# Last-stage weights decoded between the second block's own, kept in DRAM as float32, with two plain chunks and seven sevens

## The chip, the cores and the metric

The kernel runs on one core of a Trainium2 chip. The metric is the device time of one execution in microseconds (us), as the median of three runs. TensorE is called PE below, VectorE DVE, ScalarE ACT, GpSimd POOL and SyncE SP.

## The reference, cut to what matters

An attention over a small memory is followed by two dense blocks. All arrays are float32 in the reference; the weights arrive as 64-bit numbers, of which the kernel makes float32 itself ("decoding").

```python
x = attention(q, k, v, phi)                  # 2304 tokens x 512
x = (x @ w_a) * (x @ w_b) @ w_out            # first block, 512 -> 1536 -> 512
h = x @ w_in                                 # second block, 512 -> 2048
g = h * (1.0 / (1.0 + np.exp(-1.702 * h)))
out = g @ moe2_w_out                         # last stage, 2048 -> 512
```

## The kernel before, in words

Every product is made to nearly float32 accuracy by splitting both operands into a high and a low part: ACT copies the value into the reduced format (`hi`), DVE or POOL subtracts that from the value (`lo`), and PE multiplies three times (`PASSES`: high by high, low by high, high by low). The split is `hi_lo`; its subtraction is `combine`, which goes to DVE or POOL. All splits therefore carry line 339 (the subtraction) or 345 (the high part), and are told apart by their tiles.

The order of the instructions on each engine is not written by hand: streams (Python generators) ask an `Order` object for an engine, a slot or a mark, and its table of estimated times and the priorities (`PR`, `PT` and so on) decide which stream is recorded next. On the chip each engine then runs its own list strictly in that order.

The second block ("second block" below is `x @ w_in`) runs as 24 rounds (`quad`, line 1281), each of seven products of a Strassen-like scheme (`seven` makes the operands). Its weights come in 8 groups (`("in", g)`), two raw pieces each. A raw piece of 512 KB is loaded by SP into one of two `raw` tiles, decoded by two ACT instructions (lines 438 and 442) and one DVE instruction (line 444) into a `dm` tile, and combined and split into `win`. The result of a round is gated by ACT (line 1333) and stored to DRAM (`g2d`).

The last stage reads `g2d` back in 9 chunks of 256 tokens. A chunk is done in one of two ways:

- plain (`proj2`, line 1482): two tiles of 128 tokens, 16 slices of the weights, three passes, 96 matmuls of 512 columns. It needs the split weights `wo2[0..15]` and split pieces of the chunk (`sb`, 128x512 each, four for each tile). There are six slots for split pieces, `sb_s`. `QUARTERS` lists the pieces: a quarter of the weights (4 slices) at a time over all plain tiles.
- seven products (`proj2_seven`, line 1513): 168 matmuls of 256 columns. It needs also the 32 combined and split weight blocks `wt` (8 pairs, four blocks each; `load_pair` reads two 128x512 slices of float32 weights from `w2d` in DRAM, `combine` makes four 128x256 sums one after the other, and `split_t` splits each), and 14 split pieces of sums for each chunk (`sums_gated`).

Before, chunks 0 to 2 are plain and run side by side (`NF = 3`), chunk 3 is plain too (`NQ = NS = 4`), and chunks 4 to 8 use seven products. The 16 raw pieces of the last weights (`("o2", c)`) come after all those of the second block. Each is decoded, split into `wo2[c]` straight from the decode tile, and stored to `w2d`. The `wt` work waits for the mark `decoded`, which is set when `wo2[15]` is ready. The wide loads (1 MB) of the first seven-product chunk go to memory that the plain pieces occupy, so they wait until the last plain piece is split (mark `front`).

Of the kernel before, what the change touches and what calls it, by code (L numbers as in the profile page):

```python
# [15 lines left out]
HI, LO = 0, 1  # L16
# [8 lines left out]
PR = 30  # L25
PT = 28
MBN = 8
# [17 lines left out]
PY = 5  # L45
RX = 12

FIRST = (
# [147 lines left out]
def tile_mem_attention_moe_moe2(  # L196
# [127 lines left out]
    def f32(ap):  # L324
        return ap.bitcast(F32)
# [73 lines left out]
    def rows(w, r0, nr, c0, cw):  # L399
        return w[r0 * P:(r0 + nr) * P, 2 * c0:2 * (c0 + cw)].rearrange("(r p) f -> p r f", p=P)  # L400
# [4 lines left out]
    for g in range(NG1):  # L405
        for r in range(2 * NHG):
            pieces.append((("wab", g, r), 0, [rows(w, r, 1, g * CW, CW) for w in (w_a, w_b)], 1))
    pieces += [(("o1", c), 0, [rows(w_o1, c, 1, 0, DM)], 1) for c in range(F1 // P)]
    for g in range(NG2):
        pieces += [(("in", g), i, [rows(w_in, 2 * i, 2, g * G2 * P, G2 * P)], 2) for i in range(2)]  # L410
    pieces += [(("o2", c), 0, [rows(w_o2, c, 1, 0, DM)], 1) for c in range(F2 // P)]
    decoded = {}
# [16 lines left out]
    def decode_piece(t, i, name, part, n, m):  # L429
# [18 lines left out]
        if name[0] == "wab":  # L448
            wt[name] = m
            od.mark(t, *name)  # L450
        elif name[0] == "in":
            decoded[name, part] = m
            od.mark(t, "decoded", name, part)
            if part == 1:
# [617 lines left out]
    yc, win, wo2 = {}, {}, []  # L1072
    win_s, hb_s, f_s, fw_s, sb_s, tb_s = Slots(), Slots(), Slots(), Slots(), Slots(), Slots()
    wo2_t, blocks = {}, []
# [93 lines left out]
    def room_last():  # L1168
# [16 lines left out]
        for p in range(F2 // P // 2):  # L1185
            od.spawn(PT, load_pair(p))
        for c, x in enumerate(views(acc, FN, 2, n), len(pieces) - 3):
            yield "mark", "raw", c
            give(f_s, [x])
        t = yield "mark", "wo2", F2 // P - 1  # L1190
        crowded()
        od.mark(t, "decoded")
        give(tb_s, [x[0].rearrange("p f j -> p (f j)").bitcast(F32) for x in raw_t])
        yield "mark", "front"
        wide = views(acc, 2 * FN, 3, n)
        give(fw_s, wide[:2])
        yield "mark", "sw", NQ, 0, A22
        give(fw_s, wide[2:])
# [3 lines left out]
        give(fw_s, views(acc, 2 * FN, 1))  # L1202
        for x in raw_t:
            give(dm_s, views(x[0].rearrange("p f j -> p (f j)").bitcast(F32), DM, 2))

# [134 lines left out]

    NF, NQ, NS, NW = 3, 4, 4, NT // NB

# [13 lines left out]
    QUARTERS = [(i, o) for o in range(0, 4 * K4, K4) for i in range(NF)]  # L1356
    QUARTERS += [(i, o) for i in range(NF, NQ) for o in range(0, 4 * K4, K4)]

    def load_gated():
        for i, o in QUARTERS:  # L1360
            s = yield "slot", f_s
            yield from gated_part(s, i, o, o + K4)
        for i in range(NQ, NW):
# [13 lines left out]
    def split_gated():  # L1377
# [8 lines left out]
        od.mark(t, "front")  # L1386
        for i in range(NQ, NW):
            yield from (split_whole(i) if i < NS else sums_gated(i))

    def split_whole(i):  # L1390
        for h in (0, 2 * K4):
            t = yield "mark", "f", i, h
            slot, f = loaded.pop(("f", i, h))
            for o in range(0, 2 * K4, K4):
                for s in range(2):
                    yield from split_part(t, f[:, o:o + K4, s * P:(s + 1) * P], "sb", i, h + o, s)
            for o in range(0, 2 * K4, K4):
                for s in range(2):
                    t = max(t, (yield "mark", "sb", i, h + o, s))
            fw_s.release(slot, t)  # L1400

# [8 lines left out]
    def sums_gated(i):  # L1410
# [21 lines left out]
        for h in (0, 2 * K4):  # L1432
# [3 lines left out]
            fw_s.release(parts[h][0], t)  # L1436

    def load_pair(p):

# [56 lines left out]
    def proj2_seven(i):  # L1496

        if i == NS:
            for p in range(2 * K4):
                yield "mark", "wt", p  # L1500
# [86 lines left out]
    def main():  # L1587
# [20 lines left out]
        for i in range(NF, NW):  # L1608
            yield from (proj2([(i, 0), (i, 1)]) if i < NS else proj2_seven(i))

# [70 lines left out]
```

## Time and profile before

| | |
|---|---|
| median of 3 runs | 746.86 us (745.54 to 747.1) |
| profiled execution | 744.51 us |
| its span, first to last instruction | 742.7 us |
| granted TensorE clock, mean | 0.999 |
| busy share of PE, DVE, ACT, POOL | 99%, 72%, 58%, 52% |
| DMA | 153.53 MB, mean 207 GB/s |

The profiled execution is 2.35 us shorter than the median of the runs. A busy PE is not a PE at its peak: matmuls overlap, so the duration of one (389 ns for 512 columns) is longer than the distance from one to the next, which has to be worked out from starts and counts.

### The profile page before, as it was taken

Reading aid. Unit: us, or ns where it says so; the run is one execution under the profiler, and the core shown is the slowest. Engines: PE = TensorE matmul, PEld = TensorE weight load, DVE = VectorE, ACT = ScalarE, POOL = GpSimd, SP = SyncE. Lnnn points to the kernel's source line nnn. Section 1 sums busy time; section 2 is a strip of 40 time slices with the busy share of each in tenths; the row PEclk is TensorE's granted clock in tenths of the full one; section 3 lists DMA queues with packets and bytes.
Section 4 is the critical chain, followed back from the end, with each engine's and each line's share of the span. In section 5 each row is a group of like instructions: output and inputs, shape, how many; then the busy total and the mean of one; then the engine's idle time right before and its main releaser. Section 6 shows DMA issues by size and latency. Waiting matters only on the chain.

```text
span 742.7 us, 14507 instructions
## 1 busy us (share of the span) xinstructions
PE 732.1 (99%) x5344; PEld 682.7 (92%) x5344; DVE 533.2 (72%) x799; ACT 430.8 (58%) x842; POOL 386.1 (52%) x347
## 2 busy tenths in 40 slices
PE   9899999999999999999999999999999999999997
PEld 8787888888889999999999999999998888999997
DVE  2987777568983447945898666666665697898884
ACT  3678664667863456546866655565656654544441
POOL 0324366447996616914998621333240296776660
PEclk9999999999999999999999999999999999999999
DMA  8998954786778966676525575544699954544411
GB/s 276 343 327 254 322 190 160 224 280 231 256 237 264 313 195 170 171 211 191 186 100 163 180 227 162 163 136 150 210 377 301 328 157 138 189 143 143 143 26 33
DMA packets 110359, 153.53 MB, mean 207 GB/s; under 512 B 8400, under 2 KB 89040, under 8 KB 110288
## 3 DMA queue, kind: packets, MB, share of 16 engines
q1 hardware_dynamic: 104928, 143.13, 60.3%
q10 hardware_dynamic: 5360, 9.47, 3.9%
q8 instruction: 42, 0.69, 0.4%
q14 instruction: 29, 0.24, 0.1%
HBM read 100.01 MB, written 52.56 MB: 205 GB/s over the span
## 4 chain that ended last, share of the span: by engine, by line
PE 92%; DMA 3%; POOL 2%; DVE 2%; SPq 1%; issue 0%; ACT 0%; DVEq 0%; POOLq 0%
PE bank L1281 24%; PE bank L844 21%; PE bank L1006 16%; PE bank L1513 14%; PE bank L1482 12%; PE bank L792 3%; DMA q<-in_q_dram 1%; PE bank L590 1%; DMA raw_p<-in_moe_w_b_dram 1%; DMA kv<-in_k_dram 1%; PE bank L509 1%; POOL w L339 1%; SPq L372 1%; POOL attn L339 1%; DVE attn L339 0%
## 5 line engine op out<-in xcount | busy, mean ns | idle before, releaser
L844 PEld LDWEIGHTS bank<-attn,eff 128*128 128x128 f32 x1152 | 154.3, 188 | 16.2 <-issue 6.1
L844 PE MATMUL bank<-attn,eff 128*128 128x288 f32 x1152 | 163.1, 298 | 0.5 <-DVE eff L812 0.5
L339 POOL TENSOR_TENSOR acc<-acc 128x512 f32<-128x512 f32 (+2 forms) x65 | 95.0, 1481 | 68.2 <-DVE w L339 27.9
L1323 DVE TENSOR_TENSOR acc<-bank,acc 128x384 f32<-128x384 f32 x168 | 89.8, 553 | 46.3 <-PE bank L1281 40.8
L339 DVE TENSOR_TENSOR w<-acc,w 128x512 fp32r<-128x512 f32 (+2 forms) x100 | 105.0, 1076 | 20.5 <-ACT w L345 20.4
L345 ACT ACTIVATE w<-acc 128x512 fp32r<-128x512 f32 (+2 forms) x129 | 74.9, 590 | 65.7 <-PE bank L1513 38.9
L345 ACT ACTIVATE attn<-acc 128x768 fp32r<-128x768 f32 (+2 forms) x80 | 61.0, 769 | 54.5 <-PE bank L1006 38.7
L1006 PE MATMUL bank<-attn,w 128*128 128x384 f32 x504 | 91.8, 335 | 0.8 <-DVE attn L339 0.7
L1006 PEld LDWEIGHTS bank<-attn,w 128*128 128x128 f32 x504 | 87.5, 188 | 2.0 <-DVE attn L339 1.4
L339 DVE TENSOR_TENSOR attn<-acc,attn 128x768 fp32r<-128x768 f32 (+2 forms) x54 | 65.6, 1225 | 31.9 <-ACT attn L345 30.8
L1333 ACT ACTIVATE acc<-acc 128x384 f32<-128x384 f32 x96 | 49.3, 524 | 44.0 <-DVE acc L1323 43.0
L339 POOL TENSOR_TENSOR attn<-acc,attn 128x768 fp32r<-128x768 f32 (+2 forms) x26 | 41.9, 1623 | 35.8 <-ACT attn L345 35.8
L1281 PE MATMUL bank<-attn,w 128*128 128x384 f32 x288 | 55.1, 334 | 0.0
L339 POOL TENSOR_TENSOR w<-dm,w 128x256 fp32r<-128x256 f32 x27 | 24.5, 908 | 57.9 <-ACT w L345 57.9
L888 POOL TENSOR_TENSOR gr<-gr 128x288 f32<-128x288 f32 x48 | 44.6, 931 | 17.0 <-issue 7.0
L339 POOL TENSOR_TENSOR w<-acc,w 128x256 fp32r<-128x256 f32 (+2 forms) x27 | 30.0, 1119 | 44.4 <-ACT w L345 44.3
L1281 PEld LDWEIGHTS bank<-attn,w 128*128 128x128 f32 x288 | 50.4, 188 | 0.0
L1006 PE MATMUL bank<-attn,w1b 128*128 128x384 f32 x252 | 47.6, 336 | 0.2 <-DVE attn L339 0.2
L339 POOL TENSOR_TENSOR sT<-sT,sm 128x576 f32<-128x576 f32 (+1 forms) x12 | 13.5, 1126 | 64.0 <-DVE sm L654 31.7
L1281 PE MATMUL bank<-w1b,w 128*128 128x384 f32 x224 | 46.2, 334 | 0.0
L1006 PEld LDWEIGHTS bank<-attn,w1b 128*128 128x128 f32 x252 | 43.8, 188 | 0.9 <-DVE attn L339 0.5
L1281 PE MATMUL bank<-w 128*128 128x384 f32 x224 | 43.8, 334 | 0.0
(185 smaller groups left out, 1448.9 us busy)
## 6 DMA issues: line engine op xcount, KB each, us to landing
acc<-g1d SPq DMA_DIRECT2D x63, 384.0 KB, 3.8
g2d<-acc SPq DMA_DIRECT2D x96, 192.0 KB, 2.0
raw<-in_moe_w_out_dram SPq DMA_DIRECT2D x24, 512.0 KB, 4.9
acc<-g2d SPq DMA_DIRECT2D x10, 1024.0 KB, 7.6
raw<-in_moe_w_in_dram SPq DMA_DIRECT2D x16, 512.0 KB, 4.3
acc<-g2d SPq DMA_DIRECT2D x16, 512.0 KB, 5.5
g1d<-gr SPq DMA_DIRECT2D x12, 576.0 KB, 4.9
g1d<-acc SPq DMA_DIRECT2D x8, 576.0 KB, 4.8
```

The source lines that it names most:

```text
L339: (nc.gpsimd if e == POOL else nc.vector).tensor_tensor(out=dst, in0=in0, in1=in1, op=op)
L345: nc.scalar.activation(out=hi, in_=src, func=AF.Copy)
L372: nc.sync.dma_start(out=dst.rearrange("p (n f) w -> p n (f w)", n=runs), in_=src)
L792: nc.tensor.matmul(ps[c][0][row(h), :], bdv[b][half, h, :], wt["wab", g, h][0][half, :], start=True, stop=True)
L844: nc.tensor.matmul(dst[:, :U], e[:, c, sw, i * CW + j * P:i * CW + (j + 1) * P], attn(b, mv, c, u * U, U), start=(n == 0), stop=(n == 3 * ...
L888: nc.gpsimd.tensor_tensor(out=dst, in0=in0, in1=in1, op=ALU.subtract)
L1006: nc.tensor.matmul(ps[0][:, :N2], w1_of(a, g, sw)[:, r * P:(r + 1) * P], b[0][:, mv, i], start=(first and q == n == 0), stop=(q == NG1 // ...
L1281: nc.tensor.matmul(ps[0][:, :N2], w[:, sw, r, :], y[mv][r], start=(n == 0), stop=(n == 5))
L1323: nc.vector.tensor_tensor(out=s[0], in0=ps[0][:, :N2], in1=x[0], op=ALU.add)
L1333: nc.scalar.activation(out=c[0], in_=c[0], func=AF.Gelu_apprx_sigmoid)
L1482: nc.tensor.matmul(ps[i, s][0], b[0][:, sw, c - o, :], wo2[c][:, mv], start=(c == n == 0), stop=(c == 4 * K4 - 1 and n == 2),)
L1513: nc.tensor.matmul(ps[name][0][:, :NB], x[0][:, sw, c, :], moving(b, h // 2 + c, mv), start=(h == c == n == 0), stop=(h > 0 and c == K4 - ...
```

## The change

Chunks 0 and 1 are plain, chunks 2 to 8 use seven products (`NF = 2`; `NQ`, `NS` and `split_whole` go). The raw pieces of the last weights are put between those of the second block (`BETWEEN`: four after group 2, three after groups 3 to 6). A decoded piece is not split any more but stored to `w2d` by SP. When all second-block pieces are decoded, `load_last` reads the 16 slices back as float32 by SP, into the four halves of the two `raw` tiles, and `split_last` splits them into `wo2`. The `wt` work has priority `PT = 4.5` instead of 28 and no longer waits for `decoded`.

```diff
-PT = 28
+PT = 4.5
+BETWEEN = (0, 0, 4, 3, 3, 3, 3, 0)
...
+    last_rows = [(("o2", c), 0, [rows(w_o2, c, 1, 0, DM)], 1) for c in range(F2 // P)]
     for g in range(NG2):
         pieces += [(("in", g), i, [rows(w_in, 2 * i, 2, g * G2 * P, G2 * P)], 2) for i in range(2)]
-    pieces += [(("o2", c), 0, [rows(w_o2, c, 1, 0, DM)], 1) for c in range(F2 // P)]
+        for _ in range(BETWEEN[g]):
+            pieces.append(last_rows.pop(0))
...
         elif name[0] == "o2":
-            c = name[1]
-            t = max(t, (yield "mark", "room", *name))
-            t, _ = yield ACT, t, act(DM)
-            nc.scalar.activation(out=wo2[c][:, HI], in_=m[0], func=AF.Copy)
-            nc.scalar.dma_start(out=w2d[c * P:(c + 1) * P, :], in_=m[0])
-            od.mark(t + 2500.0, "w2d", c)
-            t2 = yield from combine(t, wo2[c][:, LO], m[0], f32(wo2[c][:, HI]), ALU.subtract, DM)
-            dm_s.release(m, max(t + 2500.0, t2))
-            od.mark(t2, "wo2", c)
+            nc.sync.dma_start(out=w2d[name[1] * P:(name[1] + 1) * P, :], in_=m[0])
+            t = od.store(t, P * DM * 4)
+            od.mark(t, "w2d", name[1])
+            dm_s.release(m, t)
...
-    NF, NQ, NS, NW = 3, 4, 4, NT // NB
+    NF, NW = 2, NT // NB
...
+    def load_last():
+        for c in range(F2 // P):
+            yield "mark", "w2d", c
+        give(wb_s, wide_raw())
+        for c in range(F2 // P):
+            t = max((yield "mark", "room", "o2", c), (yield "mark", "w2d", c))
+            s = yield "slot", wb_s
+            nc.sync.dma_start(out=s[0], in_=w2d[c * P:(c + 1) * P, :])
+            od.load(max(t, s[1]), P * DM * 4, "o2", c)
+            od.spawn(PR, split_last(c, s))
...
+    def split_last(c, s):
+        t = yield "mark", "o2", c
+        t = yield from hi_lo(t, wo2[c][:, HI], wo2[c][:, LO], s[0], DM)
+        wb_s.release(s, t)
+        od.mark(t, "wo2", c)
...
-        t = max((yield "mark", "pair", p), (yield "mark", "decoded"))
+        t = yield "mark", "pair", p
```

The change moves what stands on DVE and ACT around the last rounds and the plain chunks. First DVE, from the late plain pieces to the first sums of the seven-product chunks. Here `w_1713<-acc 128x512` is the low part of a split piece of a chunk, a 128x256 row is `wt` work, and `acc<-acc 128x4x128` is a sum of the first seven-product chunk. Before:

```order
L339 TENSOR_TENSOR w_1713<-acc,w_1713 128x512
L339 TENSOR_TENSOR w_1713<-raw_74,w_1713 128x256
L339 TENSOR_TENSOR w_1713<-raw_73,w_1713 128x256
L339 TENSOR_TENSOR w_1713<-acc,w_1713 128x512
L339 TENSOR_TENSOR w_1713<-raw_74,w_1713 128x256
L339 TENSOR_TENSOR w_1713<-acc,w_1713 128x512 x4
L339 TENSOR_TENSOR acc<-acc 128x4x128
```

Before, the `wt` work on DVE ends with the third 128x256 row, and the last three plain pieces and the first piece of chunk 4 (`x4`) follow it without anything between. With the change, the same place:

```order
L340 TENSOR_TENSOR w_1713<-acc,w_1713 128x512
L340 TENSOR_TENSOR w_1713<-raw_74,w_1713 128x256
L340 TENSOR_TENSOR rest<-acc,rest 128x256
L340 TENSOR_TENSOR acc<-acc 128x256
L340 TENSOR_TENSOR w_1713<-acc,w_1713 128x512
L340 TENSOR_TENSOR w_1713<-raw_73,w_1713 128x256
L340 TENSOR_TENSOR w_1713<-raw_74,w_1713 128x256
L340 TENSOR_TENSOR acc<-acc 128x256 x2
L340 TENSOR_TENSOR w_1713<-acc,w_1713 128x256 x2
L340 TENSOR_TENSOR acc<-acc 128x256
L340 TENSOR_TENSOR w_1713<-acc,w_1713 128x256
L340 TENSOR_TENSOR acc<-acc 128x256
```

The second 128x512 row here is the last plain piece; `wt` work stands on both sides of it. Behind these rows come the first piece of chunk 2, the last `wt` row, a sum and the second piece of chunk 2:

```order
L340 TENSOR_TENSOR w_1713<-acc,w_1713 128x512
L340 TENSOR_TENSOR w_1713<-acc,w_1713 128x256
L340 TENSOR_TENSOR acc<-acc 128x4x128
L340 TENSOR_TENSOR w_1713<-acc,w_1713 128x512 x2
L340 TENSOR_TENSOR acc<-acc 128x4x128
```

On ACT the two first pair loads (`L1454 DMA acc<-w2d`, line 1445 before) stand behind the last gates in both kernels. With the change, what stands behind them is the high parts of five `wo2` slices, of two plain pieces, and of the first pairs:

```order
L1335 ACTIVATE acc<-acc 128x384
L1454 DMA acc<-w2d 128x2x512 x2
L346 ACTIVATE w1b<-raw_74 128x512
L346 ACTIVATE w1b<-raw_73 128x512
L346 ACTIVATE w_1713<-acc 128x512
L346 ACTIVATE w1b<-raw_73 128x512
L346 ACTIVATE w1b<-raw_74 128x512
L346 ACTIVATE w_1713<-acc 128x512
L346 ACTIVATE w1b<-acc 128x256 x3
```

The pairs' own rows (`w1b<-acc 128x256`) have moved forward to here; before, they stood behind the sixteenth slice of the last weights.

## Rows read from the trace of the kernel before

**Rows 1.** The page, parts 1 and 4: PE's share, and the chain that ended last.
```profile
PE 732.1 (99%) x5344; PEld 682.7 (92%) x5344; DVE 533.2 (72%) x799; ACT 430.8 (58%) x842; POOL 386.1 (52%) x347
...
PE 92%; DMA 3%; POOL 2%; DVE 2%; SPq 1%; issue 0%; ACT 0%; DVEq 0%; POOLq 0%
```

**Rows 2.** Busy time by stretch: two of the plain chunks, two of the sevens.
```profile
core 0: us, PE busy (x) PEld busy (x) DVE busy (x) ACT busy (x) POOL busy (x), PEclk, DMA share, GB/s
550.50:593.00 42.50, 42.50 (x189) 35.17 (x189) 23.11 (x36) 24.19 (x46) 4.74 (x5) 1.00 0.98 326
593.00:637.60 44.60, 44.60 (x199) 36.92 (x198) 35.82 (x42) 22.64 (x52) 32.11 (x34) 1.00 0.60 178
637.60:657.80 20.20, 20.20 (x170) 20.20 (x169) 19.36 (x20) 9.62 (x16) 16.20 (x11) 1.00 0.49 155
```

**Rows 3.** Timeline of PE (start us, us, engine, line): plain chunks begin, sevens begin, last group.
```profile
550.51 9.72 PE L1482 MATMUL bank<-eff,w 128*128 128x512 f32 x42
...
637.59 0.52 PE L1513 MATMUL bank<-w1b,w 128*128 128x256 f32 x3
...
737.30 1.24 PE L1513 MATMUL bank<-w1b,w 128*128 128x256 f32 x9
```

**Rows 4.** Busy time by stretch in the second block.
```profile
440.00:460.00 20.00, 20.00 (x117) 20.00 (x116) 12.52 (x23) 11.63 (x25) 5.99 (x8) 1.00 0.54 175
...
540.00:550.50 10.50, 10.50 (x62) 10.50 (x61) 9.11 (x15) 8.13 (x17) 6.85 (x6) 1.00 1.06 391
```

**Rows 5.** Groups by line (busy us, mean ns), 540 to 645 us: decoding.
```profile
L442 ACT ACTIVATE raw<-raw 128x512 uint32<-128x512 uint8 x10 | 6.5, 652 | 0.0
...
L444 DVE SCALAR_TENSOR_TENSOR dm<-dm,raw 128x512 uint32<-128x512 uint32 x7 | 4.8, 690 | 11.8 <-ACT raw L442 11.8
L438 ACT ACTIVATE dm<-raw 128x512 f32<-128x512 f32 x7 | 4.6, 662 | 11.3 <-issue 6.6 <-DMA raw<-in_moe_w_out_dram 4.6
```

**Rows 6.** Timeline of ACT, then of POOL, around the end of the second block.
```profile
550.86 0.96 ACT L1333 ACTIVATE acc<-acc 128x384 f32<-128x384 f32 x2
556.36 2.04 ACTq L1445 DMA_DIRECT2D acc<-w2d  x2
558.45 0.67 ACT L438 ACTIVATE dm<-raw 128x512 f32<-128x512 f32 x1 [6.62 <-issue]
...
562.32 0.90 POOL L339 TENSOR_TENSOR acc<-acc 128x256 f32<-128x256 f32 x1 [12.57 <-DMA acc<-w2d]
```

**Rows 7.** Timeline of DVE from the pairs to the first pieces of chunk 4.
```profile
587.57 0.42 DVE L339 TENSOR_TENSOR acc<-acc 128x256 f32<-128x256 f32 x1
589.41 0.69 DVE L339 TENSOR_TENSOR w<-acc,w 128x512 fp32r<-128x512 f32 x1 [1.42 <-ACT w L345]
...
590.37 0.96 DVE L339 TENSOR_TENSOR w1b<-acc,w1b 128x256 fp32r<-128x256 f32 x1
...
594.24 1.23 DVE L339 TENSOR_TENSOR w<-acc,w 128x512 fp32r<-128x512 f32 x1
...
623.82 2.42 DVE L339 TENSOR_TENSOR w<-acc,w 128x512 fp32r<-128x512 f32 x3
632.47 0.69 DVE L339 TENSOR_TENSOR w<-acc,w 128x512 fp32r<-128x512 f32 x1 [6.23 <-ACT w L345]
633.19 1.67 DVE L339 TENSOR_TENSOR acc<-acc 128x512 f32<-128x512 f32 x1
```

**Rows 8.** Busy time in the stretch in which the pairs are worked on.
```profile
589.40:623.80 34.40, 34.40 (x154) 28.48 (x153) 33.22 (x38) 21.58 (x52) 32.10 (x35) 1.00 0.54 157
```

**Rows 9.** Timeline of SP, then of ACT: the load for the first seven-product chunk.
```profile
626.26 5.25 SPq L1350 DMA_DIRECT2D acc<-g2d  x4
...
631.80 1.15 ACT L345 ACTIVATE w<-acc 128x512 fp32r<-128x512 f32 x2 [9.35 <-DMA acc<-g2d]
```

**Rows 10.** Line 1445, pair loads.
```profile
DMA to landing us min/median/max: 3.4/4.3/5.6
```

**Rows 11.** PE's waits, longest first (in all, times, longest).
```profile
PE bank L549 <- POOL et L540: 1.7, 1, 1.7
```

More of the change, by code (lines that the diff above doesn't have):

```diff
@@ L408, in tile_mem_attention_moe_moe2 @@
     pieces += [(("o1", c), 0, [rows(w_o1, c, 1, 0, DM)], 1) for c in range(F1 // P)]
+    last_rows = [(("o2", c), 0, [rows(w_o2, c, 1, 0, DM)], 1) for c in range(F2 // P)]
     for g in range(NG2):
         pieces += [(("in", g), i, [rows(w_in, 2 * i, 2, g * G2 * P, G2 * P)], 2) for i in range(2)]
-    pieces += [(("o2", c), 0, [rows(w_o2, c, 1, 0, DM)], 1) for c in range(F2 // P)]
+        for _ in range(BETWEEN[g]):
+            pieces.append(last_rows.pop(0))
+    assert not last_rows
     decoded = {}
@@ L453, in decode_piece @@
             od.mark(t, "decoded", name, part)
+            if (name[1], part) == (NG2 - 1, 1):
+                od.spawn(PR, load_last())
             if part == 1:
@@ L1072, in tile_mem_attention_moe_moe2 @@
     yc, win, wo2 = {}, {}, []
-    win_s, hb_s, f_s, fw_s, sb_s, tb_s = Slots(), Slots(), Slots(), Slots(), Slots(), Slots()
+    win_s, hb_s, f_s, fw_s, sb_s, tb_s, wb_s = (Slots() for _ in range(7))
     wo2_t, blocks = {}, []
@@ L1186, in room_last @@
             od.spawn(PT, load_pair(p))
-        for c, x in enumerate(views(acc, FN, 2, n), len(pieces) - 3):
-            yield "mark", "raw", c
+        for c, x in enumerate(views(acc, FN, 2, n), F2 // P - 3):
+            yield "mark", "o2", c
             give(f_s, [x])
@@ L1192, in room_last @@
         od.mark(t, "decoded")
+        for _ in range(4):
+            yield "slot", wb_s
         give(tb_s, [x[0].rearrange("p f j -> p (f j)").bitcast(F32) for x in raw_t])
@@ L1196, in room_last @@
         give(fw_s, wide[:2])
-        yield "mark", "sw", NQ, 0, A22
+        yield "mark", "sw", NF, 0, A22
         give(fw_s, wide[2:])
@@ L1202, in room_last @@
         give(fw_s, views(acc, 2 * FN, 1))
-        for x in raw_t:
-            give(dm_s, views(x[0].rearrange("p f j -> p (f j)").bitcast(F32), DM, 2))
+        give(dm_s, wide_raw())
     def split(t, dst, src, n, *key):
@@ L1356, in tile_mem_attention_moe_moe2 @@
     QUARTERS = [(i, o) for o in range(0, 4 * K4, K4) for i in range(NF)]
-    QUARTERS += [(i, o) for i in range(NF, NQ) for o in range(0, 4 * K4, K4)]
     def load_gated():
@@ L1362, in load_gated @@
             yield from gated_part(s, i, o, o + K4)
-        for i in range(NQ, NW):
+        for i in range(NF, NW):
             for o in (0, 2 * K4):
@@ L1386, in split_gated @@
         od.mark(t, "front")
[L1387 to L1400, printed above, removed]
+        for i in range(NF, NW):
+            yield from sums_gated(i)
     A21 = 7
@@ L1436, in sums_gated, with wide_raw @@
             fw_s.release(parts[h][0], t)
+    def load_last():
[8 more added lines that the diff above has]
+            od.spawn(PR, split_last(c, s))
+    def wide_raw():
+        return [y for x in raw_t for y in views(x[0].rearrange("p f j -> p (f j)").bitcast(F32), DM, 2)]
+    def split_last(c, s):
[3 more added lines that the diff above has]
+        od.mark(t, "wo2", c)
     def load_pair(p):
@@ L1496, in proj2_seven @@
     def proj2_seven(i):
-        if i == NS:
+        if i == NF:
             for p in range(2 * K4):
@@ L1608, in main @@
         for i in range(NF, NW):
-            yield from (proj2([(i, 0), (i, 1)]) if i < NS else proj2_seven(i))
+            yield from proj2_seven(i)
     def quad(g, p):
```

## The prediction

> **What bounds the kernel now.** I read the page's head and the chain that ended last first: PE is busy 99% of the span and carries 92% of the chain [rows 1], and its longest single wait in the whole program is 1.7 us, early on [rows 11]. So the time is the sum of what PE is given, and an edit pays only if it takes work from PE without making it wait. Then I read the stretches of the last stage [rows 2]: PE is full in all of them, but DVE and POOL are not the same in each. In the first half of the plain chunks POOL does 4.74 us in 42.5; in the second half, where the 32 weight blocks are made, DVE is busy 35.8 and POOL 32.1 of 44.6 us. In the first seven-product chunk DVE is at 19.4 of 20.2. There is a wide, loosely filled stretch before a full one, and the full one ends about 11 us before PE needs its result: DVE's last plain piece ends at 626.2 [rows 7], PE begins the sevens at 637.6 [rows 3]. The change takes about half of that stretch away.
>
> **What PE saves.** PE starts the plain chunks at 550.51 and the sevens at 637.59 [rows 3]: 87.08 us for 4 chunks x 96 = 384 matmuls, 226.8 ns each, 21.77 us a chunk. The last group of nine starts at 737.30 and lasts 1.24, so the five other chunks take 637.59 to 738.54, 100.95 us for 840 matmuls, 120.2 ns each, 20.19 us a chunk. One chunk that changes its form saves 1.58 us, two save 3.2 us. I take the pitch from starts and counts, since a matmul's own duration overlaps the next.
>
> **Decoding moves into the second block.** Sixteen pieces bring two ACT instructions of 0.66 us and one DVE instruction of 0.69 us each [rows 5]: 21 us on ACT, 11 on DVE, over the five groups between which they stand, some 110 us (15 rounds of 42 matmuls, 7.2 us each at 117 in 20 us [rows 4]). DVE works there 12.5 and ACT 11.6 of 20 us [rows 4]; with 2.0 and 3.8 us more per 20 neither is full, and PE covers it. Their raw loads move with them. The stretch from 540 has a DMA share of 1.06 and the first half of the plain chunks 0.98, but the second block only 0.54 [rows 2, 4]. The extra 4 MB that are read back from `w2d` (16 slices of 256 KB) fall near the end of the block, where the raw loads have gone. Cost nothing; if the cover were gone, a round would wait for its `win` weights (a rival below).
>
> **The joint before the sevens.** This is where the change can lose. PE, unhindered, would end two plain chunks at 550.51 + 192 x 0.2268 = 594.06. What is late next is the first piece of chunk 2. Its 1 MB load goes to memory that the last plain piece occupies. Before, the last plain piece was subtracted by 626.24 (623.82 + 2.42), SP issued the load at 626.26 [rows 9], ACT took the first high part at 631.80, and the first low part ended at 632.47 + 0.69 = 633.16 [rows 7]: 6.92 us from piece to piece. This costs nothing before, as PE had until 637.59. With the change, the last plain piece must be done by 594.06 - 6.92 = 587.1, or PE waits.
>
> When is it done? The pair work cannot start earlier than before by much: ACT stands still from the last gate (551.82) to 558.45, for the issue of the two pair loads, which wait for the stores of the last rounds; the first pair was worked on at 562.32 [rows 6]. Before, this stop was harmless. Now the high parts of five `wo2` slices are queued behind it on ACT, and DVE waits for these. From the first pair instruction to the last plain piece, inclusive, DVE has by the order 24 subtractions of 256 and 10 of 512. Their price hangs on POOL. With POOL idle, one of 256 takes 0.42 us and one of 512 takes 0.69; with POOL busy on the same kind of work 0.96 and 1.23 [rows 7]. Bounds: 24 x 0.42 + 10 x 0.69 = 17.0 us and 24 x 0.96 + 10 x 1.23 = 35.3 us, that is, an end at 579.3 or at 597.6. The nearest row is the same work before: 38 DVE instructions in 34.4 us beside 35 of POOL [rows 8], 0.905 us each, which gives 34 x 0.905 = 30.8 and an end at 593.1. I take 592.0, near that row: POOL has only some 22 instructions in that time against 35, so some of DVE's go at the short price (which alone would bring the end forward by up to 5 us), but there are new waits in line. Pairs 2, 3, 6 and 7 are loaded into the room of earlier pairs, 4.3 us each from issue to landing [rows 10], and the issue sits in ACT's list between high parts, so a late pair holds up a plain piece.
>
> So PE's first wait is 592.0 - 587.1 = 4.9 us. A second one follows: behind the first piece DVE does a block (0.42), a sum (1.67 [rows 7]) and the second piece (0.69), 2.8 us, while PE uses up the first piece in 12 x 0.120 = 1.4 us: 1.3 us more. After that the seven-product chunks run as before; DVE has 17 to 19 of 20 us to do in them, which fits.
>
> Here a rule of the Trainium skill can be weighed. The row on short and long prices says that the same instruction takes 0.42 or 0.96 us [rows 7]. The page VectorE: DVE Perf Modes (The TRN2 errata) gives float32 tensor-tensor work as (N + 151) / 0.96 ns, 424 ns for 256 and 691 for 512, which the rows with POOL idle confirm; by it alone the queue would take 17.1 us, PE would not wait, and the kernel would gain its 3.2 us. The GPSIMD Engine Reference (Key points) says that GpSimd shares its SBUF interfaces with VectorE and contends with VectorE instructions of two SBUF inputs; that speaks against this change, and the long rows agree with it.
>
> **The sum.** -3.2 + 4.9 + 1.3 = +3.0 us. On the profiled execution's 744.51 us (span 742.7 and 1.8 around it) this is 747.5 us. The median of the runs is 2.35 us above that execution, so the forecast for the median is **749.9 us**.
>
> **The rivals.**
>
> *DVE keeps up* (ends on the other side). The mechanism is the short price: POOL has a third less to do beside each DVE instruction, and DMA is freer after 550, so the pair loads land sooner than 4.3 us and ACT's stop of 6.6 us shrinks. For it: the 3.4 us minimum of a landing [rows 10], the 0.42 us rows. Against it: DVE's 33.2 busy of 34.4 us before [rows 8]. It decides if the last plain piece is done before 587.1; then nothing but the second wait is left, and the time is 746.86 - 3.2 + 0 to 1.3 = 743.7 to 745.0.
>
> *The wait eats the gain*: the last piece ends between 587.5 and 590.5, the wait is 1.7 to 4.7 with the second one, the result within 1.5 us of 746.9.
>
> *The queue is slow throughout*: all DVE instructions at the long price, end at 597.6, wait 10.5 + 1.3, +8.6 us, 755.5. For it: long rows were the rule while both worked. Against: POOL's smaller share.
>
> *A second-block round waits for its weights.* The groups share two raw tiles and few `dm` tiles with the new pieces, and by the order the last high part of group 3 stands one round later than before. It costs only if it slips by a further round (7.2 us); DVE and ACT have 7 and 8 of 20 us free [rows 4]. Price 1 to 5 us on top, 748 to 755.
>
> *PE's clock falls in the wait.* The granted clock is 1.00 in every stretch [rows 2], but no row shows a PE wait of 5 us, so no row shows what one does. If it fell to half, each 1.4 us piece of the first products would take 2.9 us; two such pieces add 2.9 us, 752.8. TensorE: Matmul & The Clock Gate of the Trainium skill (What's actually happening) says that an idle engine goes back to half the clock; no run here shows it.
>
> **How the numbers follow.** What a measurement of this kernel can tell from no change is about 0.2%, 1.5 us. The forecast's mechanism with an end of the last plain piece later than 590.5 has 0.45; the slow queue, a late round or a fallen clock 0.12 together; so slower has 0.57. The cancelled gain has 0.20. DVE keeping up has 0.23. The range reaches from 743.7, where nothing waits, to 754.0, which leaves out the far end of the slow queue and of the late rounds. The forecast's own range, for an end at 590.5 to 594.5, is 748.4 to 752.4.
>
> **What would show it.** Right: 192 matmuls of line 1482 at 227 ns and 1176 of line 1513 at 120; a PE wait of 3 to 6 us between the two, released by ACT or DVE, with the load from `g2d` ahead of it and the last plain piece's subtraction ahead of that; a small second one behind; ACT idle for some 6 us at 552; no new PE waits between 380 and 550. Wrong: PE running from the plain chunks into the sevens without a gap (then the short price held), several 1 us waits inside the plain chunks instead (then pieces, not the load, were late), or a wait within the second block.

## The result, and the profile after

The changed kernel takes 750.13 us (median of 5 runs, 749.62 to 750.53) against 746.86 (745.54 to 747.10): ratio 1.0055, 95% interval 1.0039 to 1.0071. It is slower by 3.3 us, which is clear of the noise. The 746.86 rests on three executions; measured again beside the experiments (17 to 23 executions each time), the kernel before has medians of 745.31 to 746.84. The profiled executions differ by more: 750.13 (span 748.3) against 744.51 (span 742.7), 5.6 us. The rows below are of the profiled ones. Its page, parts 1 and 4:

```profile
PE 732.1 (98%) x5488; PEld 688.2 (92%) x5488; DVE 549.1 (73%) x825; ACT 434.6 (58%) x852; POOL 410.9 (55%) x363
...
PE 22%; DMA 4%; DVE 4%; ACT 1%; issue 1%; POOL 1%; ACTq 0%; SPq 0%; DVEq 0%
```

PE's busy time is the same as in [rows 1] although it has two chunks in the cheaper form. The 22% can't be set against the 92% of [rows 1]: the shares add up to a third, as the page follows this chain back only to 497.65 us. What it shows is where the chain leaves PE (start us, us, what):

```profile
561.93 6.82 DMA acc<-w2d
...
601.12 0.61 DVE w L340
601.78 142.62 PE bank L1522 x1174
```

From the end back to 601.78 the chain is PE. From there back to the landing of a pair's load at 568.75 it is DVE's list, with a few rows of ACT between. PE's timeline has the waits (start us, us, engine, line; in brackets the idle time ahead of a row and what ended it). The second block, the plain products, the sevens and the last group:

```profile
375.69 1.03 PE L1283 MATMUL bank<-eff,w 128*128 128x384 f32 x5
...
552.70 0.63 PE L1491 MATMUL bank<-eff,w 128*128 128x512 f32 x2
...
584.70 11.75 PE L1491 MATMUL bank<-w1b,w 128*128 128x512 f32 x51
600.89 0.51 PE L1522 MATMUL bank<-w1b,w 128*128 128x256 f32 x2 [4.44 <-ACT w L346]
601.78 0.58 PE L1522 MATMUL bank<-w1b,w 128*128 128x256 f32 x1 [0.38 <-DVE w L340]
...
743.15 1.24 PE L1522 MATMUL bank<-w1b,w 128*128 128x256 f32 x9
```

The busy time by stretch, with the granted clock as the third column from the end and the DMA share behind it; the first row answers to one of [rows 4]:

```profile
440.00:460.00 20.00, 20.00 (x117) 20.00 (x117) 13.11 (x24) 14.52 (x32) 8.19 (x10) 1.00 0.73 232
...
375.69:552.70 177.01, 175.97 (x1009) 174.58 (x1009) 127.13 (x222) 115.29 (x249) 86.07 (x91) 1.00 0.71 232
...
596.40:600.90 4.50, 0.06 (x2) 0.01 (x1) 4.50 (x7) 3.06 (x8) 4.31 (x5) 1.00 1.08 364
600.90:606.00 5.10, 4.72 (x25) 4.51 (x26) 5.10 (x7) 4.87 (x10) 3.09 (x2) 0.67 0.76 226
```

Read these as an account from [rows 3]. The plain products begin at 552.70 and not at 550.51: +2.2. Two chunks in the cheaper form: -3.2. At 226.8 ns each, 192 plain matmuls end at 596.25; the sevens begin at 600.89: +4.6. From there 1176 matmuls at 120.2 ns would end at 742.24; the last ends at 744.39 (743.15 + 1.24): +2.15, of which 0.38 is a second, short wait. The other 1.8 lie at 600.9 to 606, where PE is busy and gets 25 matmuls done in 5.1 us, at a mean granted clock of 0.67. The sum is +5.8, as the spans say (+5.6).

What stands ahead of the first wait, in the timelines of ACT, POOL, DVE, SP and ACT again, answers to [rows 6, 7, 9]. A row with a count can hold two shapes and shows the first: the `x2` at 601.05 is the first piece's low part and a 128x256 block.

```profile
558.34 3.96 ACTq L1454 DMA_DIRECT2D acc<-w2d  x2
562.34 1.15 ACT L346 ACTIVATE w1b<-raw 128x512 fp32r<-128x512 f32 x2 [6.68 <-DMA acc<-w2d]
...
598.20 2.64 POOL L340 TENSOR_TENSOR w<-acc,w 128x256 fp32r<-128x256 f32 x3
...
566.02 0.41 DVE L340 TENSOR_TENSOR acc<-acc 128x256 f32<-128x256 f32 x1
...
592.97 0.85 DVE L340 TENSOR_TENSOR w<-acc,w 128x512 fp32r<-128x512 f32 x1 [0.31 <-ACT w L346]
...
601.05 2.10 DVE L340 TENSOR_TENSOR w<-acc,w 128x512 fp32r<-128x512 f32 x2
603.07 0.68 DVE L340 TENSOR_TENSOR acc<-acc 128x512 f32<-128x512 f32 x1
603.67 2.38 DVE L340 TENSOR_TENSOR w<-acc,w 128x512 fp32r<-128x512 f32 x2
...
593.84 0.99 SPq L1352 DMA_DIRECT2D acc<-g2d  x2
...
600.22 1.44 ACT L346 ACTIVATE w<-acc 128x512 fp32r<-128x512 f32 x3
```

ACT stands still for 6.7 us behind the last gate, over the two pair loads; the last plain piece is done at 593.82, SP issues the load at 593.84, and ACT takes the first high part of the sevens at 600.22. The pairs' work begins on DVE at 566.02.

### The profile page after: what moved, and what is told of

It reads as the page before. It is cut to its first block, busy times and chain, and to the rows that moved or that the text cites. A ratio compares the mean times of both kernels' runs of the same rounds, so it can differ in the third digit from the quotient of the medians.

```text
span 748.3 us, 14926 instructions
## 1 busy us (share of the span) xinstructions
PE 732.1 (98%) x5488; PEld 688.2 (92%) x5488; DVE 549.1 (73%) x825; ACT 434.6 (58%) x852; POOL 410.9 (55%) x363
## 5 line engine op out<-in xcount | busy, mean ns | idle before, releaser
L340 POOL TENSOR_TENSOR acc<-acc 128x512 f32<-128x512 f32 (+2 forms) x80 | 118.8, 1507 | 60.0 <-DVE w L340 38.9
L340 DVE TENSOR_TENSOR w<-acc,w 128x512 fp32r<-128x512 f32 (+2 forms) x118 | 125.2, 1089 | 16.8 <-ACT w L346 16.7
L346 ACT ACTIVATE w<-acc 128x512 fp32r<-128x512 f32 (+2 forms) x146 | 84.8, 588 | 77.6 <-PE bank L1522 55.1
L1325 DVE TENSOR_TENSOR acc<-bank,acc 128x384 f32<-128x384 f32 x168 | 87.4, 550 | 31.6 <-PE bank L1283 17.8
L346 ACT ACTIVATE attn<-acc 128x768 fp32r<-128x768 f32 (+2 forms) x84 | 62.5, 752 | 55.7 <-PE bank L1007 39.6
L1007 PEld LDWEIGHTS bank<-attn,w 128*128 128x128 f32 x504 | 87.5, 188 | 2.0 <-DVE attn L340 1.4
L340 POOL TENSOR_TENSOR w<-dm,w 128x256 fp32r<-128x256 f32 x33 | 30.0, 914 | 59.5 <-ACT w L346 59.5
L1335 ACT ACTIVATE acc<-acc 128x384 f32<-128x384 f32 x96 | 46.9, 517 | 17.3 <-DVE acc L1325 16.9
L1283 PEld LDWEIGHTS bank<-attn,w 128*128 128x128 f32 x288 | 50.4, 188 | 0.5 <-ACT acc L1318 0.5
L1522 PE MATMUL bank<-attn,w 128*128 128x256 f32 x336 | 50.1, 285 | 0.0
L340 POOL TENSOR_TENSOR w<-acc,w 128x256 fp32r<-128x256 f32 (+2 forms) x26 | 27.1, 1052 | 32.8 <-DVE dm L448 18.4
L1522 PEld LDWEIGHTS bank<-attn,w 128*128 128x128 f32 x336 | 45.0, 194 | 0.0
```

What stands on the lines that cost most here:

```text
L340: (nc.gpsimd if e == POOL else nc.vector).tensor_tensor(out=dst, in0=in0, in1=in1, op=op)
L346: nc.scalar.activation(out=hi, in_=src, func=AF.Copy)
L1007: nc.tensor.matmul(ps[0][:, :N2], w1_of(a, g, sw)[:, r * P:(r + 1) * P], b[0][:, mv, i], start=(first and q == n == 0), stop=(q == NG1 // ...
L1283: nc.tensor.matmul(ps[0][:, :N2], w[:, sw, r, :], y[mv][r], start=(n == 0), stop=(n == 5))
L1325: nc.vector.tensor_tensor(out=s[0], in0=ps[0][:, :N2], in1=x[0], op=ALU.add)
L1335: nc.scalar.activation(out=c[0], in_=c[0], func=AF.Gelu_apprx_sigmoid)
```

## The experiments

Each kernel is the changed one with the edit shown. To tell the parts apart I take three figures from each trace: how long the second block is (from its first product to the first plain one), how long the rest is (from there to the end of the span), and what PE waits for at the joint. Before: 174.7 and 192.2. After: 177.0 and 195.6. With two plain chunks and nothing lost, the rest would be 192.2 - 3.2 = 189.0. The ratio is to executions of the kernel before that were measured together with the run: medians of 746.84 (e1 to e4), 745.31 (e5 to e8), 745.59 (e9 to e11) and 746.34 (e12). The parts are of one profiled execution each.

| run | time, us | ratio to before (95%) | second block | rest | PE's waits at the joint |
|---|---|---|---|---|---|
| e1_early | 754.75 | 1.0111 (1.0094 to 1.0128) | 176.6 | 199.1 | 0.1, 2.2, 3.2, 0.8 |
| e2_filler | 751.95 | 1.0075 (1.0054 to 1.0096) | 177.4 | 194.2 | 0.4, 0.3 |
| e3_three_plain | 745.10 | 0.9983 (0.9969 to 0.9997) | 175.0 | 190.5 | none |
| e4_rows_behind | 767.64 | 1.0289 (1.0268 to 1.0310) | 174.9 | 191.1 | none; 21.9 ahead of the plain products |
| e5_thin_rows | 750.24 | 1.0058 (1.0040 to 1.0076) | 174.7 | 194.2 | 3.2, 0.4 |
| e6_third_pair | 758.35 | 1.0164 (1.0144 to 1.0184) | 177.8 | 201.8 | 0.6, 0.6, 3.3, 5.3 |
| e7_no_pair_lows | 746.13 | 0.9996 (0.9983 to 1.0009) | 176.4 | 189.1 | 0.1 |
| e8_three_spread | 746.13 | 0.9997 (0.9984 to 1.0010) | 174.7 | 190.5 | none |
| e9_spread | 753.27 | 1.0095 (1.0078 to 1.0111) | 175.9 | 197.6 | 5.9, 0.7 |
| e10_vector_alone | 747.86 | 1.0023 (1.0010 to 1.0036) | 177.2 | 191.1 | 0.1, 0.2, 0.7, 0.2 |
| e11_alone_and_spread | 745.38 | 1.0000 (0.9984 to 1.0015) | 175.6 | 188.8 | none |
| e12_alone_third_late | 746.08 | 0.9995 (0.9982 to 1.0009) | 174.7 | 190.6 | 0.1, 0.8, 0.2 |

### e1: the load ahead of the last plain piece

```diff
-        give(f_s, views(acc, FN, 1, n + 2 * FN))
+        give(f_s, views(acc, FN, 2, n))
...
-        give(fw_s, wide[:2])
-        yield "mark", "sw", NF, 0, A22
-        give(fw_s, wide[2:])
+        give(fw_s, wide[:1])
...
+    def room_wide(wide):
+        for k in (1, 2):
+            for j in range(2):
+                yield "mark", "sb", NF - 1, 4 * k, j
+            give(fw_s, [wide[k]])
```

> The last plain pieces go to the lower memory, so that the two 1 MB loads of the first seven-product chunk need no memory of the last plain piece and can be under way before it is split. Theory A (the wait at the joint is the load that stands behind the last plain piece, 593.84 to 600.2): TensorE's wait of 4.4 us falls to under 1 us, the granted clock stays at 1.00 there, the second wait of 0.4 goes; 750.1 - 4.4 - 0.4 - 1.7 = 743.6, between 743 and 745.5. Theory B (VectorE and GpSimd are themselves late by then, and would be as late with the operands loaded): the low parts of the first product start where they do now, about 601, the wait stays over 3 us and the time at 749 to 750.5.

Theory A fell. Theory B holds in kind and not in size: the time is 4 us above its range. The sevens do begin without a wait, at 596.12, and then PE stands inside the first product (PE, then POOL, then a stretch of this run with the granted clock third from the end; its lines are two higher):

```profile
601.16 0.51 PE L1524 MATMUL bank<-w 128*128 128x256 f32 x2 [2.24 <-POOL w L340]
604.92 0.58 PE L1524 MATMUL bank<-w 128*128 128x256 f32 x1 [3.25 <-ACT w L346]
606.29 0.79 PE L1524 MATMUL bank<-w 128*128 128x256 f32 x2 [0.80 <-POOL w L340]
...
598.21 2.90 POOL L340 TENSOR_TENSOR w<-acc,w 128x256 fp32r<-128x256 f32 x3
601.08 3.16 POOL L340 TENSOR_TENSOR acc<-acc 128x256 f32<-128x256 f32 x3
604.20 2.04 POOL L340 TENSOR_TENSOR w<-acc,w 128x256 fp32r<-128x256 f32 x2
...
602.00:612.00 10.00, 6.29 (x27) 6.00 (x28) 9.96 (x11) 3.81 (x8) 7.35 (x7) 0.51 0.55 157
```

What is late are the weight blocks of the last pairs, 128x256 rows: low parts end at 601.11 (PE goes on at 601.16) and 606.24 (606.29), and between them, at 604.92, PE gets the high part of a block whose sum POOL ends at 604.24. The first product needs a block of every pair. In the changed kernel the last such row on POOL ends at 598.20 + 2.64 = 600.84, where PE's wait ends too. So two things were late by the same amount, the load behind the last piece and the pairs, and the trace names only the last of them. In e1 the pairs come 5.4 us later: DVE has first sums to do before the pairs are finished, and ACT issues the load of the last pair at 595.64 instead of 591.89. The clock adds to the loss: it stays at half for some 10 us, where the changed kernel is back at 1.00 from 606 on (rows under e2). So e1 shows which operands were late, and not what an early load alone is worth.

### e2: work for PE in the wait

```diff
+        t, ps = yield PE, 0.0, 220, bank_m
+        for _ in range(34):
+            nc.tensor.matmul(ps[0][:, :NB], wo2[0][:, HI, :P], wo2[0][:, HI, :NB], start=True, stop=True)
+        bank_m.release(ps, t)
         for i in range(NF, NW):
             yield from proj2_seven(i)
```

> 34 products of 256 columns on operands already there, into a bank nobody reads, between the last plain product and the first of the seven: 34 x 0.12 = 4.1 us of TensorE work inside its wait of 4.4. The sevens' operands are as late as before. Theory A (the granted clock falls because TensorE stood still, 0.50 at 602 to 604, and this costs about 1.7 us behind the wait): the first sevens run at 1.00, the time is 750.1 - 1.7 = 748.4. Theory B (the thin stretch behind the wait is operands that come late, not the clock): no change, 749.7 to 750.5.

The clock in 2 us steps, first of the changed kernel, then of this run:

```profile
602.00:604.00 2.00, 2.00 (x10) 2.00 (x11) 2.00 (x3) 1.77 (x5) 1.03 (x2) 0.50 0.53 124
604.00:606.00 2.00, 2.00 (x15) 2.00 (x14) 2.00 (x3) 2.00 (x5) 1.50 (x1) 0.73 0.87 289
606.00:608.00 2.00, 2.00 (x19) 2.00 (x18) 2.00 (x4) 1.12 (x3) 1.27 (x1) 1.00 1.07 384
```

```profile
600.00:602.00 2.00, 2.00 (x18) 1.88 (x17) 2.00 (x4) 2.00 (x6) 1.43 (x2) 1.00 1.08 337
602.00:604.00 2.00, 1.64 (x12) 1.29 (x11) 2.00 (x3) 1.70 (x5) 0.83 (x1) 1.00 0.55 111
604.00:606.00 2.00, 1.69 (x14) 1.63 (x14) 2.00 (x3) 2.00 (x5) 1.60 (x1) 1.00 1.00 325
```

What PE still waits for in this run:

```profile
603.55 0.50 PE L1522 MATMUL bank<-w 128*128 128x256 f32 x2 [0.36 <-ACT w L346]
604.37 0.86 PE L1522 MATMUL bank<-w 128*128 128x256 f32 x5 [0.31 <-DVE w L340]
```

That PE stood still is what lowered the clock: with work in the wait it stays at 1.00. From the first seven to the last, less the waits in it, the changed kernel takes 143.1 us (743.15 + 1.24 - 600.89 - 0.38) and this run, whose last group also lasts 1.24 and starts at 742.82, 142.0 (less 601.41, 0.36 and 0.31), against 141.35 at the pitch of [rows 3]. The fall cost 1.1 to 1.8 us. The rest of the execution is 1.4 us shorter, as theory A has it. The median of 751.95 is above the ranges of both theories. This profile is the fastest of six executions (749.82 to 755.13); the five others ran at a mean clock of 0.997 or 0.998 against 1.000, so it fell somewhere in them too, and no trace shows where. Shown for the clock in one execution, open for the time.

### e3: three plain chunks

```diff
-    NF, NW = 2, NT // NB
+    NF, NW = 3, NT // NB
```

> Three chunks plain side by side and six in sevens: 65.3 us of cover for the pairs and the splits instead of 43.5. Theory A (the pairs, the splits and the load need a fixed time of about 41 us plus 8 us for the third chunk's pieces plus 6 to 7 us for the load, about 57 us behind the block's end): no wait at the joint and no fall of the clock, the second block still ends 2.2 us late, 1.6 us of the saving lost: 750.1 - 6.5 + 1.6 = 745.2, between 744 and 746.5. Theory B (VectorE and GpSimd work through the pieces no faster than TensorE through the plain products, so that the wait moves along): a wait of 3 to 5 us stays and the time is 751 to 752.

Theory A, to 0.1 us in the time. One part was wrong: the second block is not late any more, although the rows stand in it as before. That asked for an explanation, which e12 gives.

### e4 and e5: which part of the rows delays the second block

e4 has `BETWEEN = (0, 0, 0, 0, 0, 0, 0, 16)`. e5 loads an eighth of each row:

```diff
                 dst = s[0][:, i * m:(i + 1) * m, :]
+                if pieces[n][0][0] == "o2":
+                    dst, src = dst[:, :m // 8], src[:, :, :m // 4]
```

> All sixteen last-stage rows decoded behind the second block's own, as the kernel before had them, the detour over DRAM kept. Theory A (the rows in between delay ScalarE and VectorE in the second block's middle, and so TensorE): the second block ends at about 550.5 instead of 552.7, and the small waits around 484 to 509 are gone; the rows come back from DRAM later, so that a wait of up to 10 us may stand at the start of the plain products or at the joint: 748 without one, 750 to 758 with one. Theory B (the block's later end has to do with the stores and the loads of the detour, wherever they are): the block ends at 552 or later.

> Of each of the sixteen last-stage rows only an eighth is loaded (64 KB for 512 KB; the decoding works on whatever else stands in its tile, so the last stage's weights are not the reference's). All instructions of the engines stay. Theory A (the second block ends late because 8 MB more go through the DMA queue beside it: its share is 0.74 at 466 to 514 against 0.45 before, and the block's own rows land late, 5.9 us): the block ends at 550.5 to 551.3 and the time is 748 to 749. Theory B (the decoding itself, 2 us of ScalarE and VectorE for each row in the line ahead of what TensorE waits for): the block ends at 552.3 or later and the time is 749.6 to 750.6.

In e4 the block has its old length, as theory A has it, and PE then waits 21.9 us for the rows to come back from DRAM, twice what I had expected at most; the time is 10 us above the range. In e5 all instructions of ACT and DVE remain, and so do the stores to `w2d` and the loads from it; seven eighths of the raw loads go, and the block takes 174.7 us: the decoding alone delays nothing. The time did not follow (750.24 lies in theory B's range), since this execution's joint still waits 3.2 us and the second block began 3.0 us later than after (the last section has the place where it fell behind).

### e6: a place for a third pair

```diff
-        give(tb_s, views(acc, 2 * DM, 2))
+        give(tb_s, views(acc, 2 * DM, 2) + views(acc, 2 * DM, 1, n + FN))
...
-        for c, x in enumerate(views(acc, FN, 2, n), F2 // P - 3):
+        for c, x in enumerate(views(acc, FN, 1, n), F2 // P - 3):
```

> A third place for a pair's 512 KB, in memory that stands unused there, so that three pairs are loaded ahead instead of two. Theory A (the joint waits for the pairs; VectorE and GpSimd stand without work between the first pairs and the next, GpSimd 573 to 577, because the third pair can't be loaded): about 3 us of that idle time goes, the wait falls from 4.4 to 1 to 2 us, with it some of the clock's fall: 746 to 748.5. Theory B (from the first pair on the two engines have work all the time, so that it is their rate alone): no change, 749.5 to 750.5.

758.35 us, 8 us above both ranges. This says nothing of either theory: as the edit stands, the third place comes back into use for a late pair after its memory has been given to the first 1 MB load, so that part of the operands is overwritten. PE waited 3.3 and 5.3 us there.

### e7 and e10: the work of VectorE and GpSimd

```diff
     def split_t(t, dst, src, p, i):
-        t = yield from hi_lo(t, dst[:, HI], dst[:, LO], src, DM // 2)
+        t, _ = yield ACT, t, act(DM // 2)
+        nc.scalar.activation(out=dst[:, HI], in_=src, func=AF.Copy)
```

> The low parts of the 32 combined blocks are not computed (the products that use them multiply what the memory holds). This takes 32 instructions of 0.9 us from VectorE and GpSimd, some 14 us of each, and leaves every load, store and product. Theory A (the joint waits for the work of VectorE and GpSimd): no wait at the joint and no fall of the clock, 750.1 - 4.8 - 1.7 = 743.6, between 743 and 745. Theory B (the joint waits for transfers: the pairs' loads that need the places of earlier pairs, and the 1 MB load): the wait stays at 2 us or more, 746.5 or more.

```diff
-        both = {POOL: Lengths.pool * pool(n), DVE: Lengths.both * dve(n)}
+        both = {DVE: dve(n)} if Lengths.alone else {POOL: Lengths.pool * pool(n), DVE: Lengths.both * dve(n)}
...
         short()
+        Lengths.alone = True
...
-        crowded()
```

> In the last stage every subtraction and low part goes to VectorE, none to GpSimd. An operation on 128x256 starts 0.34 us after the one before it on VectorE while GpSimd is idle, and 0.88 while GpSimd works too, so that the two together need 0.44 for each. Theory A (the joint is late by the two engines' rate, and they slow each other): 64 x 0.34 + 16 x 0.60 + 5 x 0.60 = 34 us from 563, the last at 597 to 598 instead of 600.8; the wait falls to 1 to 2 us and the clock hardly falls: 745.5 to 747.5. Theory B (GpSimd's share is a real help): VectorE has 29 more operations to do and the joint waits longer: 751 to 756.

Theory A at the joint in both, and both times above its range. e7's rest is 189.1, so next to nothing is lost at the joint. Its time is 2.5 us above the 743.6 that I expected (the late second block is already in that figure): in the profiled execution the block began 2.7 us later, and the two shortest of its twelve executions, at a mean clock of 1.000, took 743.48 and 743.82. e10 does all the work and loses 2.1 us at the joint instead of 6.6; its 747.86 is 0.4 above theory A's range and 3 below theory B's. Its edit also drops `crowded()`, which lengthens times in the table that orders the lists, so that their order changes too. The price itself is read from ten microseconds among the pairs, first of the changed kernel, then of e10:

```profile
580.00:590.00 10.00, 10.00 (x46) 8.29 (x45) 10.00 (x12) 6.20 (x16) 10.00 (x11) 1.00 0.10 38
```

```profile
580.00:590.00 10.00, 10.00 (x45) 8.28 (x45) 10.00 (x27) 7.36 (x19) 0.00 (x0) 1.00 0.45 151
```

DVE and POOL together did 23 instructions, DVE alone 27, in each case four of 128x512 and the others of 128x256. The groups by line of e10 in that stretch give 0.42 us for one of 128x256 and 0.68 for 128x512, where DVE beside POOL took 0.96 and 1.23 [rows 7]:

```profile
L342 DVE TENSOR_TENSOR raw<-raw 128x256 f32<-128x256 f32 x8 | 3.3, 419 | 0.0
L342 DVE TENSOR_TENSOR w<-acc,w 128x512 fp32r<-128x512 f32 x4 | 2.7, 682 | 0.0
```

DMA traffic is not what makes the difference: its share is 0.10 in the slow stretch and 0.45 in the quick one.

### e8, e9 and e11: the rows spread over six groups

```diff
-BETWEEN = (0, 0, 4, 3, 3, 3, 3, 0)
+BETWEEN = (0, 2, 3, 3, 3, 3, 2, 0)
```

e8 has it with three plain chunks, e9 alone, e11 with e10's edit.

> Three plain chunks, and the sixteen rows spread over six groups of the second block (0, 2, 3, 3, 3, 3, 2, 0) instead of five. Theory A (the block's later end comes of too much in too short a time): it ends within 0.5 us of the kernel before (550.5), the time is 744 to 744.8. Theory B (each row costs its part wherever it is put, or the early rows delay groups that have no slack): 745 to 747.

> The changed kernel with its sixteen rows spread over six groups of the second block, (0, 2, 3, 3, 3, 3, 2, 0) instead of (0, 0, 4, 3, 3, 3, 3, 0), and nothing else. Theory A (four rows in a group are more than the queue can carry beside that group's own loads): from its first product to its end the second block takes 174.7 us as before the change, not 177.0, the joint stays as it is: 750.1 - 2.3 = 747.8. Theory B (the rows cost the block the same wherever they are put): 177 us, 749.6 to 750.5.

> Both edits of the two runs beside it. If both theories A hold and the two losses have nothing to do with each other, the gains add: 750.1 - 2.3 - 3 to 4.5 = 743.3 to 744.8, faster than the kernel before. If only one holds, its own figure.

The block's delay goes from 2.3 to 1.2 us in e9 and 0.9 in e11. But in all three PE waits 1.5 us for POOL just ahead of the second block, at about 370, where it waited 0.5, and e9's joint came out worse, 5.9 us; why, stays open. e9's 753.27 is above both theories; the spreading is no cure by itself. In e8 the block has its old length (theory A) and the time lies in theory B's range; it tells nothing of the spreading, as e3 had lost nothing either. e11 misses the 743.3 to 744.8 of added gains: 745.38 is the time of the kernel before (1.0000). Its profiled execution is the shortest of the study, 743.24, with a rest of 188.8; its twelve runs reach up to 749.25.

### e12: one load out of the queue

With e10's edit:

```diff
-        give(f_s, views(acc, FN, 3, 2 * AN))
+        give(f_s, views(acc, FN, 2, 2 * AN))
+        yield "mark", "g2", (NG2 - 2, 0), 0, 0
+        give(f_s, views(acc, FN, 1, 2 * AN + 2 * FN))
```

> VectorE alone as in e10, and the last of the three memories that are free early for the gated sums is given out late in the second block. With two plain chunks the third load, of the first chunk's second quarter, stands in SP's line at 452.3 to 457.05 and waits for gated sums still on their way to DRAM; with three chunks (e3) that place went to the third chunk's first quarter, at 405, and its second block took 175.0 us instead of 177.0. Here the load stands behind the last of the second block's rows. Theory A (this load holds up the rows queued behind it, and so ScalarE, VectorE and TensorE at 476 to 516): the second block takes 174.7 to 175.2 us from its first product to its end, against 177.2 in e10; 747.9 - 2.2 = 745.7 in the median, 743 to 743.5 where the clock does not fall at 30 us. Theory B (the rows' own transfers delay it, this load is one more among them): 176.5 to 177.3 us, 747 to 748.5 in the median.

Theory A, in the block and in the time. SP's list of the changed kernel with ACT's wait that follows, and then of e12 (its lines are two to four higher, and its second block began 2.5 us later), and last ACT's wait in e5:

```profile
451.41 0.89 SPq L1337 DMA_DIRECT2D g2d<-acc  x1
457.05 0.37 SPq L1352 DMA_DIRECT2D acc<-g2d  x1
...
458.49 0.48 SPq L373 DMA_DIRECT2D raw<-in_moe_w_in_dram  x1
...
464.55 0.67 ACT L442 ACTIVATE acc<-raw 128x512 f32<-128x512 f32 x1 [5.54 <-DMA raw<-in_moe_w_in_dram]
```

```profile
453.96 3.87 SPq L1341 DMA_DIRECT2D g2d<-acc  x2
457.92 0.39 SPq L465 DMA_DIRECT2D w2d<-dm  x1
458.36 0.44 SPq L375 DMA_DIRECT2D raw<-in_moe_w_in_dram  x1
...
462.74 0.67 ACT L444 ACTIVATE acc<-raw 128x512 f32<-128x512 f32 x1 [1.53 <-DMA raw<-in_moe_w_in_dram]
```

```profile
465.94 0.66 ACT L444 ACTIVATE acc<-raw 128x512 f32<-128x512 f32 x1 [5.45 <-DMA raw<-in_moe_w_in_dram]
```

The row at 457.05 is the load of a plain piece. SP stands 4.7 us at it, until the gated sums that it reads have reached DRAM, and it puts 512 KB more into the queue ahead of the next raw pieces; ACT, whose list has the decoding ahead of the gates, stands 5.5 us and not 1.5. PE loses its 2.3 us in small pieces between 476 and 516 (by counts of matmuls in steps of 10 us from the block's start). The stop of ACT is not enough by itself: in e5, which has the load in the same place, it is as long (5.45 us), and the block loses nothing. It takes the load and the full rows together; e12 takes away the one, e5 the other. How the stop reaches PE was not followed row by row. `QUARTERS` lists the pieces by quarter over all plain chunks, so with three of them the third free memory goes to the third chunk's first quarter, which is ready early; with two it goes to the second quarter of the first chunk. All profiled executions with that load there and full rows in between lost 0.9 to 3.1 us in the block; e3, e8 and e12, without it, 0.0 to 0.3.

## Why the prediction came out as it did

**The saving per chunk** was right: two chunks, 3.2 us, by starts and counts.

**"Cost nothing" for the decoding in the second block** failed, by 2.3 us in the profiled execution. It was one of the rivals, but with the wrong cause (and its range of 748 to 755 does not follow from its price: 1 to 5 us on top of 749.9 are 750.9 to 754.9): I looked for a round that slips by a list position, and at busy shares of ACT and DVE, 11.6 and 12.5 of 20 us [rows 4], which still had room afterwards. I read the DMA share of 0.54 [rows 4] as cover, and did not add up what would come to it; the same stretch now shows 0.73. And I did not follow SP's list past the moved pieces: it was the shorter list of plain pieces that put a waiting load among them, and that load and the rows together made the delay.

**The first wait** was right in size, 4.9 forecast and 4.6 measured: the last plain piece was done 41.1 us behind the block's end (593.82), where I had 41.5. In part errors cancel here. The pairs' work began 13.3 us behind the block's end (566.02) and not 11.8, and DVE's 34 instructions took 27.8 us and not 29.7. From the last plain piece to the first low part of the sevens it was 7.9 us (601.73) and not 6.9, but PE began with the high part, at 600.89. The forecast's account of the wait was only half of it. The load behind that piece was one of two limits, and e1 shows that taking it away gains nothing, for the pairs were just as late. Both go back to the term on which the argument turned, the long price of DVE beside POOL, and e7 and e10 confirm that one. The GPSIMD Engine Reference of the Trainium skill (Key points) says that GpSimd shares its SBUF interfaces with VectorE and contends with VectorE instructions of two SBUF inputs; the 0.42 us of e10 without POOL and the 0.96 beside it agree, though no run shows the interfaces themselves.

**The second wait**, of 1.3 us for the second piece, did not come. The 0.38 us at 601.78 belong to the first piece: PE had begun with its high part alone and waits for its low part. Behind that DVE did a block, a sum and the second piece's low part (from 603.67), as I had said; but PE was at half clock and used up the first piece more slowly. At full clock the second wait is there: 0.36 us for the high part and 0.31 for the low part in e2, 0.76 and 0.22 in e12. So its mechanism was right, and its size is 0.7 to 1.0 us.

**PE's clock** was a rival with "no row shows what a wait of 5 us does". It fell to 0.50, that is to 1.2 of 2.4 GHz, and cost 1.1 to 1.8 us, less than the 2.9 that I had reckoned. TensorE: Matmul & The Clock Gate of the Trainium skill (What's actually happening) says that an idle engine goes back to half the clock; the rows after the wait agree, and e2, without the idle time, stays at full speed.

**The median.** The forecast of 749.9 is 0.2 us from the measured 750.13, but not for its own reasons alone. On the profiled execution the sum gave 747.5, and 750.13 was measured; the 2.6 us between are the block (+2.2), the clock (+1.8), two waits smaller by 1.2 in all, and 0.25 less from the last matmul to the span's end. I had added 2.35 us for the distance of the profiled execution from its median. By the mean clocks that distance belongs to a fall of the clock at 30 to 40 us (below), which the profiled execution of the changed kernel did not have although it is the median itself. So 2.6 us left out and 2.35 us too much cancel: that the forecast came so near is luck. In the changed kernel the mean clock does not tell the times apart: 749.79 to 750.53 us at 0.998, 749.62 and 750.39 at 0.995.

## What to carry to other kernels

Add a moved load to the queue that it is moved into, together with whatever changes its place there because a list got shorter; a busy share that looks free on the engines says nothing of what stands in line at SP. When two engines slow each other down, count what they finish together in a stretch, not how busy they are: here one of them alone was faster. And when the trace names one releaser for a wait, ask what else ended within the same tenth of a microsecond before removing it. With e10's and e12's edits the change comes back from 1.0055 to 0.9995 of the time before, no gain that can be measured; three plain chunks do as well (0.9983, interval 0.9969 to 0.9997) with a single number changed.

## What the runs showed of the hardware that was not expected

Two instructions at a time on DVE and POOL were slower than one after the other on DVE: 23 against 27 in 10 us.

The kernel before has two times: 744.4 to 746.1 us, at a mean granted clock of 0.999 or 1.000, and 746.3 to 747.7 at 0.996 to 0.998. The trace of e7 shows such a fall. At 33 us PE waits 1.69 us in the kernel before and in e7 alike. One stretch near the start and two around the wait, first of the kernel before, then of e7:

```profile
5.00:6.00 1.00, 1.00 (x12) 1.00 (x11) 0.00 (x0) 0.00 (x0) 0.00 (x0) 1.00 0.81 211
...
30.00:35.00 5.00, 3.26 (x28) 2.36 (x29) 4.96 (x14) 3.69 (x9) 3.74 (x5) 1.00 0.96 320
35.00:40.00 5.00, 5.00 (x48) 4.78 (x50) 4.31 (x12) 4.52 (x13) 1.97 (x2) 1.00 1.04 350
```

```profile
5.00:6.00 1.00, 1.00 (x7) 1.00 (x6) 0.00 (x0) 0.00 (x0) 0.00 (x0) 1.00 0.88 289
...
30.00:35.00 5.00, 3.10 (x22) 1.29 (x19) 4.96 (x15) 2.60 (x6) 2.94 (x4) 0.91 0.86 283
35.00:40.00 5.00, 5.00 (x32) 5.00 (x31) 3.40 (x11) 3.79 (x11) 2.51 (x3) 0.75 1.04 353
```

After the same wait of PE the clock falls in one execution and not in the other, and the second block begins at 378.43 instead of 375.79. The fall is not all of these 2.6 us: e7 is 1.1 us late already when the wait ends (33.89 against 32.81). e4, e5, e10 and e12 have the same fall at the same place, and begin at 378.0 to 378.8. In these five the stretch from 5 to 6 us has 7 matmuls, in the nine profiled executions without the fall 10 to 12; why a slower start goes with the fall is not shown. No row of the kernel before itself shows the fall, so that its two times are a conclusion from the mean clocks.
